# Eight sums of the numerator moved from VectorE to accumulating transfers inside SBUF, in a kernel of attention and a rational MLP

## The chip, the cores and the metric

One core of one Trainium2 chip runs the whole program as one launch. The metric is device microseconds from the start to the end of an execution, the median over the runs shown. The profile is one more execution of the same program, taken with the hardware profiler.

## The reference, cut to what matters

The input is q, k and v of 8 batches, 8 heads, 576 positions and 64 channels. Each head gets a banded attention (a position sees its neighbours at a distance below 4) and a second attention over positions averaged in groups of four; their sum is the MLP's input, 4608 tokens by 512 channels. The MLP has a rational function between its two products:

```python
def _moe_ref(x, w_in, w_out, a, b):
    h = x @ w_in                                   # 4608 x 2048
    h2 = h * h
    h3 = h2 * h
    P = a[0] + a[1] * h + a[2] * h2 + a[3] * h3
    Q = 1.0 + np.abs(b[0]) * np.abs(h) + np.abs(b[1]) * h2
    g = P / (Q + 1e-06)
    return g @ w_out
```

All is float32.

## The kernel before, in words

**The MLP.** The tokens go in nine blocks of 512: one of each batch's first 512 positions, and one of the 64 positions that are left of each batch. A block takes sixteen steps, one for each 128 of the 2048 inner columns, so there are 144 steps, n = 0 to 143; the third block has the steps 32 to 47. A step has three parts:

- TensorE makes h, 128 x 512, in one of two PSUM banks that take turns (line 1090): 12 matmuls, four each of high input with high weights, low input with high weights and high input with low weights. Each float32 factor is split in a high and a low part, so that their three products give the precision of float32.
- `middle` makes g out of h. ScalarE (line 1103) reads the bank four times: |b0 h| into tb, h squared into tq, a3 h + a2 into ta, and a1 h + a0 into u. VectorE makes the denominator, tb = b1 tq + tb (line 1147), and ta = ta tq (line 1152). The last sum of the numerator is ta = ta + u (line 1156). ScalarE takes the logarithm of tb + 1 into log and its negative exponential into tq, which is the reciprocal of the denominator. VectorE then makes the high part gh = ta tq (line 1182), the error of it, tb = (tb + 1) gh (line 1187) and ta = ta - tb (line 1196), and the low part gl = ta tq (line 1182 again).
- `o_part` multiplies g with the output weights into four banks that gather the block's sixteen steps (line 1220): eight matmuls that read gh, with high and low weights in turn, then four that read gl.

Two sets of buffers take turns: even steps use ta = m1, tb = m3, tq = m5, gh = g1, gl = g3; odd steps m0, m2, m4, g0 and g2. u (gb1, gb0) lies in the memory of gh and log (gb3, gb2) in that of gl. So u of step n + 2 waits until TensorE has read gh of step n, and gh of a step is written over its own u.

**Attention for later blocks runs in between.** While a block's MLP runs, the attention of a later batch is worked off in two groups of two head pairs: scores into PSUM (lines 483 and 563 on TensorE), masking (497), maxima (592, 646), exponentials (627, 657 on ScalarE), sums and scaling (668, 669, 674, 692), two transposes on VectorE (779, 759) that go over DRAM and come back as eu and eq, the products with v (932, 894 on TensorE), and the sums into the next block's input (971, 975, 957, 1050). The averages of q, k and v over four positions (pq, vq) are made by transfers: SyncE loads the first of four, and GpSimd's queue adds the other three with accumulating transfers from DRAM (line 444), each of which waits until the one before it on the same tile has landed.

**The order is planned.** Every piece of work is a task with an engine, a planned cost and a due time. A planner in the kernel simulates the five engines, takes on each the most urgent task that is ready, and so writes one fixed order for each engine; the program is emitted in that order, and the engines work it off in order, with semaphores between them. A table of offsets (SHIFT) moves single tasks' due times. An accumulating transfer inside SBUF is already known to the planner through `added`; it stands on GpSimd's queue, with an issue cost of 0.93, a wait of 2.05 and a load of ADD_LOAD = 1.3 in the planner's units:

```python
def added(x, y):
    add(
        "POOL", 0.93, lambda: nc.gpsimd.dma_start(out=x.ap, in_=y.ap, accum_op=ALU.add),
        (x, y), (x,), load=ADD_LOAD,
    )
```

`middle` uses it for the sum of line 1156 in the steps that ADD_DMA names, of which there are none before the change.

Of the kernel before, what the change touches and what calls it, by code (L numbers as in the profile page):

```python
# [76 lines left out]
class Plan:  # L77
# [16 lines left out]
    def add(self, engine, dur, fn, reads=(), writes=(), due=None, load=None, at=0.0, wait=2.05, big=False, more=None):  # L94
        t = Task()
        t.engine, t.dur, t.fn, t.due, t.n, t.load, t.at = engine, dur, fn, due, len(self.tasks), load, at
        t.preds, t.succs, t.late, t.start = {}, [], 1e9, None
        t.key, t.wait, t.big, t.more = self.key, wait, big, more
        self.key = t.key[0], t.key[1] + 1
        rk = set().union(*(r.keys for r in reads)) if reads else set()  # L100
        wk = set().union(*(w.keys for w in writes)) if writes else set()
        for k in rk | wk:
            w = self.writer.get(k)
            if w is not None:
                t.preds[w] = True
        for k in wk:
            for r in self.readers.get(k, ()):
                t.preds.setdefault(r, False)
            self.writer[k] = t
            self.readers[k] = []  # L110
        for k in rk - wk:
            self.readers.setdefault(k, []).append(t)
        t.preds.pop(t, None)
        for p in t.preds:
            p.succs.append(t)
        self.tasks.append(t)
        return t
# [91 lines left out]
def attention_moe(  # L209
# [895 lines left out]
# [5 lines that stand above are left out]
# [26 lines left out]
    def middle(n):  # L1136
# [15 lines left out]
        add("DVE", 0.602, lambda: v.tensor_tensor(out=ta.ap, in0=ta.ap, in1=tq.ap, op=ALU.mult), (ta, tq), (ta,))  # L1152
        if n in ADD_DMA:
            added(ta, u)
# [321 lines left out]
ET_DVE = ()  # L1476
MASK_LATE = 2
POOL_PE = {1: (1, 'ACT')}
ADD_DMA = range(0)
SUB_DMA = range(0)  # L1480
NEG = ()
ADD_LOAD = 1.3
# [261 lines left out]
```

## Time and profile before

| | us |
|---|---|
| median of 2 runs | 942.74 (942.63 to 942.84) |
| span of the profiled execution, first to last instruction | 944.6 |
| TensorE busy in the span | 927.3 |
| VectorE busy | 873.4 |
| ScalarE busy | 772.9 |
| GpSimd busy | 153.1 |

The profiled execution's own time is its span, 944.6 us; no other time of that execution is given, and it lies 1.9 us above the median of the runs. Busy times count an instruction from its start to its end; instructions that overlap in a pipeline have longer durations than distances (a matmul of 512 columns lasts 0.39 us and is followed by the next after 0.23 us), so distances between starts say what an engine can do.

### The profile page before, as it was taken

What the parts mean: (1) busy time and instruction counts of PE and PEld (TensorE: products, weight loads), DVE (VectorE), ACT (ScalarE), POOL (GpSimd) and SP (SyncE); (2) the same over time, 40 slices, a digit from 0 to 9 for tenths busy, and PEclk for the clock granted to TensorE, in tenths of its full rate; (3) what the DMA queues carried; (4) which work ended last, traced back from release to release, by engine and by line L of the source; (5) the groups of instructions that cost most, each with busy time, mean ns of one, the idle gap of its engine ahead of it and who ended that gap; (6) DMA issues with size and microseconds to landing.
All of it is one profiled execution on the core that took longest, in us unless ns stands there. A gap on an engine that the chain in (4) does not pass through costs nothing.

```text
span 944.6 us, 19519 instructions
## 1 busy us (share of the span) xinstructions
PE 927.3 (98%) x7011; PEld 726.4 (77%) x7011; DVE 873.4 (92%) x1549; ACT 772.9 (82%) x1943; POOL 153.1 (16%) x182
## 2 busy tenths in 40 slices
PE   9998999999999999999999999999999999999996
PEld 7655666778777878878787878887878888788885
DVE  6998999999999999999999999999999988988886
ACT  4898999997797979796989788888979776777664
POOL 2032233130302222121203030304020000000000
PEclk9999999999999999999999999999999999999999
DMA  9679855643465646575656565656633010001001
GB/s 284 249 216 245 254 114 90 190 67 116 87 151 123 136 112 140 146 134 124 131 148 116 136 122 157 111 144 112 178 63 91 1 45 1 0 1 45 1 1 45
DMA packets 93136, 109.32 MB, mean 116 GB/s; under 512 B 23120, under 2 KB 75344, under 8 KB 93040
## 3 DMA queue, kind: packets, MB, share of 16 engines
q1 hardware_dynamic: 70000, 88.01, 31.7%
q0 software_dynamic: 23040, 20.07, 15.8%
q8 instruction: 55, 0.90, 0.4%
q14 instruction: 41, 0.34, 0.1%
HBM read 87.05 MB, written 20.99 MB: 114 GB/s over the span
## 4 chain that ended last, share of the span: by engine, by line
PE 44%; DVE 25%; ACT 23%; issue 5%; DMA 1%; SPq 1%; DVEq 0%; ACTq 0%
PE psum L1220 18%; PE psum L1090 16%; ACT m L1103 10%; DVE g L1182 5%; ACT gb L1103 5%; PE psum L1078 4%; ACT el L627 3%; DVE m L1147 3%; DVE m L1152 3%; DVE m L1196 3%; DVE m L1187 3%; ACT ep L674 2%; ACT ep L657 2%; DVE nm L592 1%; DVE xf L957 1%
## 5 line engine op out<-in xcount | busy, mean ns | idle before, releaser
L1220 PE MATMUL psum<-wh,g 128*128 128x512 f32 x1152 | 370.2, 398 | 4.0 <-DVE g L1182 2.6
L1090 PE MATMUL psum<-xs,wh 128*128 128x512 f32 (+1 forms) x1040 | 262.4, 389 | 0.3
L1220 PEld LDWEIGHTS psum<-wh,g 128*128 128x128 f32 x1152 | 213.5, 188 | 60.6 <-DVE g L1182 7.7
L1103 ACT ACTIVATE m<-psum,cf 128x512 f32<-128x512 f32 x288 | 210.8, 743 | 53.0 <-PE psum L1090 41.9
L1090 PEld LDWEIGHTS psum<-xs,wh 128*128 128x128 f32 x1040 | 191.8, 188 | 43.2 <-ACT gb L1103 2.7
L1182 DVE TENSOR_TENSOR g<-m,m 128x512 fp32r<-128x512 f32 x288 | 194.6, 686 | 32.9 <-ACT m L1103 25.2
L1220 PE MATMUL psum<-wl,g 128*128 128x512 f32 x576 | 224.5, 391 | 0.0
L1090 PE MATMUL psum<-xs,wl 128*128 128x512 f32 (+1 forms) x520 | 138.1, 387 | 0.0
L1103 ACT ACTIVATE gb<-m 128x512 f32<-128x512 f32 x144 | 93.0, 646 | 47.7 <-DVE m L1147 39.3
L1220 PEld LDWEIGHTS psum<-wl,g 128*128 128x128 f32 x576 | 108.2, 188 | 21.3
L1103 ACT ACTIVATE gb<-psum,cf 128x512 f32<-128x512 f32 x144 | 114.0, 792 | 7.0 <-PE psum L1220 6.2
L1090 PEld LDWEIGHTS psum<-xs,wl 128*128 128x128 f32 x520 | 96.4, 188 | 20.7 <-issue 1.0
L1147 DVE SCALAR_TENSOR_TENSOR m<-m,cf,m 128x512 f32<-128x512 f32 x144 | 107.0, 743 | 5.4 <-ACT m L1103 4.3
L1103 ACT ACTIVATE m<-gb 128x512 f32<-128x512 f32 x144 | 92.7, 644 | 15.0 <-DVE m L1152 9.4
L444 POOL DMA_DIRECT2D vq<-in_vq_dram x60 | 52.3, 915 | 312.0 <-DMA vq<-in_vq_dram 260.6
L1156 DVE TENSOR_TENSOR m<-m,gb 128x512 f32<-128x512 f32 x144 | 98.6, 685 | 3.9 <-ACT gb L1103 3.1
L444 POOL DMA_DIRECT2D pq<-in_qkp_dram x84 | 73.6, 933 | 174.0 <-DMA pq<-in_qkp_dram 166.7
L1187 DVE SCALAR_TENSOR_TENSOR m<-m,g 128x512 f32<-128x512 f32 x144 | 98.9, 687 | 2.1
L1196 DVE TENSOR_TENSOR m<-m,m 128x512 f32<-128x512 f32 x144 | 98.8, 686 | 1.6
L1152 DVE TENSOR_TENSOR m<-m,m 128x512 f32<-128x512 f32 x144 | 98.4, 683 | 0.9 <-ACT m L1103 0.9
L1103 ACT ACTIVATE m<-psum 128x512 f32<-128x512 f32 x144 | 87.1, 605 | 2.0 <-DVE g L1182 1.6
L627 ACT ACTIVATE el<-el,nm 128x64 f32<-128x64 f32 x240 | 80.6, 350 | 2.6 <-DVE nm L619 2.2
(100 smaller groups left out, 884.2 us busy)
## 6 DMA issues: line engine op xcount, KB each, us to landing
qk<-in_qk_dram SPq DMA_DIRECT2D x32, 590.0 KB, 13.3
pq<-in_qkp_dram POOLq DMA_DIRECT2D x84, 144.0 KB, 3.9
vw<-in_vw_dram SPq DMA_DIRECT2D x32, 320.0 KB
out_dram<-xf SPq DMA_DIRECT2D x32, 256.0 KB, 2.5
bounce<-tt SPq DMA_DIRECT2D x96, 80.0 KB, 1.9
eu<-bounce SPq DMA_DIRECT2D x40, 160.0 KB, 3.2
sl<-in_w_out_dram SPq DMA_DIRECT2D x12, 512.0 KB, 3.6
vq<-in_vq_dram POOLq DMA_DIRECT2D x60, 96.0 KB, 3.1
```

The source lines that it names most:

```text
L444: lambda d=dst, x=src, r=r: nc.gpsimd.dma_start(out=d.ap, in_=rows(x, r), accum_op=ALU.add),
L627: nc.scalar.activation(out=s.el.ap[:, k, j, :], in_=view[:, j, k, :], func=AF.Exp, bias=nm[:, 5 * j + k : 5 * j + k + 1], scale=scale, acc ...
L1078: nc.tensor.matmul(ph.ap, lhsT=bits[0][fc].ap[:, c, :].bitcast(F32), rhs=x.ap[:, c, :], start=(c == 0), stop=(c == NCC - 1),)
L1090: nc.tensor.matmul(ph.ap[:, f * t : (f + 1) * t], lhsT=(high, low)[j][0][fc].ap[:, c, :], rhs=blk.x[i].ap[:, c, t0 : t0 + t], start=(part_ ...
L1103: add("ACT", cost, lambda: nc.scalar.activation(out=out_.ap, in_=in_, func=func, **kw), (room_in, cf, *more), (out_,))
L1147: lambda: v.scalar_tensor_tensor(out=tb.ap, in0=tq.ap, scalar=b1, in1=tb.ap, op0=ALU.mult, op1=ALU.add),
L1152: add("DVE", 0.602, lambda: v.tensor_tensor(out=ta.ap, in0=ta.ap, in1=tq.ap, op=ALU.mult), (ta, tq), (ta,))
L1156: add("DVE", 0.602, lambda: v.tensor_tensor(out=ta.ap, in0=ta.ap, in1=u.ap, op=ALU.add), (ta, u), (ta,))
L1182: return v.tensor_tensor(out=out, in0=x, in1=y, op=ALU.mult)
L1187: lambda: v.scalar_tensor_tensor(out=tb.ap, in0=tb.ap, scalar=CONE, in1=gh.ap.bitcast(F32), op0=ALU.add, op1=ALU.mult),
L1196: add("DVE", 0.602, lambda: v.tensor_tensor(out=ta.ap, in0=ta.ap, in1=tb.ap, op=op), (ta, tb), (ta,))
L1220: nc.tensor.matmul(ob[sub].ap, lhsT=g[i].ap[:, g0 : g0 + P], rhs=flat((high, low)[j][1][fc].ap), start=(fc == 0 and m == 0), stop=(fc == N ...
```

## The change

In the steps 40 to 47, the second half of the third block, ta = ta + u is no longer an instruction of VectorE. GpSimd's queue issues a transfer of 256 KB from u to ta, both in SBUF, that adds to what is there. The planner is run again with these eight tasks on the other engine, and its order changes around them.

```diff
-ADD_DMA = range(0)
+ADD_DMA = range(40, 48)
```

On VectorE eight rows of line 1156 go; on GpSimd's queue eight rows of a new line 1107 come. On all engines the order is the same up to step 40 and, but for a few neighbours that change places between the steps 118 and 123, again from step 55 on.

**GpSimd's queue.** This is where the transfers of the steps 43 to 47 stand between the accumulating loads of line 444 (pq and vq are the averages for the attention, m1 and m0 the numerators ta of even and odd steps, gb1 and gb0 their u):

```order
+L1107 DMA m0_161<-gb0_171 128x512
 L444 DMA vq1_216<-in_vq_dram 128x192
 L444 DMA vq0_215<-in_vq_dram 128x192
...
 L444 DMA vq1_216<-in_vq_dram 128x192
 L444 DMA vq0_215<-in_vq_dram 128x192
+L1107 DMA m1_162<-gb1_172 128x512
+L444 DMA pq1_203<-in_qkp_dram 128x288
+L444 DMA pq0_192<-in_qkp_dram 128x288
+L1107 DMA m0_161<-gb0_171 128x512
```

The transfers of the steps 40 to 43 stand one behind the other ahead of the six loads of vq; that of step 44 stands behind all six, and that of step 45 behind the first two loads of pq. The remaining two stand behind the other four loads of pq.

**VectorE between gh and gl of step 44.** First as it was (g1 and g3 are gh and gl of this even step, m1, m3 and m5 its ta, tb and tq; the other names are of step 45 and of the attention):

```order
L1182 TENSOR_TENSOR g1_168<-m1_162,m5_166 128x512
L592 TENSOR_REDUCE nm1_182<-el1_207 128x10
L497 TENSOR_TENSOR el0_196<-psum,maskd_178 128x128
L619 TENSOR_TENSOR nm1_182<-nm1_182,scales_180 128x10
L1187 SCALAR_TENSOR_TENSOR m3_164<-m3_164,g1_168 128x512
L592 TENSOR_REDUCE nm0_181<-el0_196 128x10
L1152 TENSOR_TENSOR m0_161<-m0_161,m4_165 128x512
L619 TENSOR_TENSOR nm0_181<-nm0_181,scales_180 128x10
L1196 TENSOR_TENSOR m1_162<-m1_162,m3_164 128x512
L1147 SCALAR_TENSOR_TENSOR m2_163<-m4_165,cf_179,m2_163 128x512
L1182 TENSOR_TENSOR g3_170<-m1_162,m5_166 128x512
```

And as it is now:

```order
L1182 TENSOR_TENSOR g1_168<-m1_162,m5_166 128x512
L668 TENSOR_SCALAR sm1_186<-sm1_186 128x13
L1152 TENSOR_TENSOR m0_161<-m0_161,m4_165 128x512
L669 RECIPROCAL sm1_186<-sm1_186 128x13
L1147 SCALAR_TENSOR_TENSOR m2_163<-m4_165,cf_179,m2_163 128x512
L692 TENSOR_TENSOR el1_207<-el1_207,sm1_186 128x640
L759 STREAM_TRANSPOSE tp1_212<-ep1_210 128x480
L1187 SCALAR_TENSOR_TENSOR m3_164<-m3_164,g1_168 128x512
L779 STREAM_TRANSPOSE tt1_204<-el1_207 128x640
L1196 TENSOR_TENSOR m1_162<-m1_162,m3_164 128x512
L1182 TENSOR_TENSOR g3_170<-m1_162,m5_166 128x512
```

The masking and maxima of the attention that stood here have moved ahead of gh, and the scaling and the two transposes that stood behind gl are now in front of it. TensorE's row has moved with it: the second four of the eight products with gh of step 44 stood ahead of the score products of line 563 and of h of step 46 before, now all eight stand behind h of step 46, six ahead of h of step 47 and two behind it.

**ScalarE at step 46.** Before, u of this step (gb1) followed its tb (m3) directly (m5 is tq, gb3 log; m2, m4 and m0 are of step 47, el0 of the attention):

```order
L1103 ACTIVATE m5_166<-psum 128x512
L1103 ACTIVATE m3_164<-psum,cf_179 128x512
L1103 ACTIVATE gb1_172<-psum,cf_179 128x512
L627 ACTIVATE el0_196,sm0_185<-el0_196,nm0_181 128x64 x5
L1103 ACTIVATE gb3_174<-m3_164 128x512
```

Now seven rows stand between them, the first of them ep0's exponential:

```order
L1103 ACTIVATE m3_164<-psum,cf_179 128x512
L657 ACTIVATE ep0_199,sm0_185<-psum,nm0_181 128x144 x3
L1103 ACTIVATE m2_163<-psum,cf_179 128x512
L1103 ACTIVATE gb3_174<-m3_164 128x512
L674 ACTIVATE ep0_199<-ep0_199,sm0_185 128x144 x3
L1103 ACTIVATE m5_166<-gb3_174 128x512
L1103 ACTIVATE m0_161<-psum,cf_179 128x512
L1103 ACTIVATE m4_165<-psum 128x512
L1103 ACTIVATE gb1_172<-psum,cf_179 128x512
```

So the last reading of step 46's PSUM bank, which h of step 48 is written to, now stands behind that step's own logarithm and exponential, behind the scaling of line 674 and behind two readings of step 47's bank.

## Rows read from the trace of the kernel before

**Rows 1.** Windows: stretch, its length, busy us (instructions) by engine, clock, DMA
```profile
core 0: us, PE busy (x) PEld busy (x) DVE busy (x) ACT busy (x) POOL busy (x), PEclk, DMA share, GB/s
321.00:372.00 51.00, 50.77 (x409) 40.92 (x408) 48.73 (x88) 42.99 (x121) 10.50 (x12) 1.00 0.61 134
...
750.00:800.00 50.00, 50.00 (x221) 41.23 (x221) 42.32 (x66) 36.15 (x60) 0.00 (x0) 1.00 0.06 22
```

**Rows 2.** Waits of TensorE's matmuls and weight loads, 321 to 380 us
```profile
PE psum L483 <- DVE el L497: 0.2, 1, 0.2
...
PEld psum L1090 <- ACT gb L1103: 0.4, 1, 0.4
```

**Rows 3.** Line 1156 in 321 to 372 us: durations, first and last start
```profile
L1156 DVE TENSOR_TENSOR m<-m,gb x8: 684/686/692, 324.5 to 367.4; 128x512 f32<-128x512 f32 x8
```

**Rows 4.** DMA issues of the whole span: KB each, median us to landing
```profile
pq<-in_qkp_dram POOLq DMA_DIRECT2D x84, 144.0 KB, 3.9
...
out_dram<-xf SPq DMA_DIRECT2D x32, 256.0 KB, 2.5
...
vq<-in_vq_dram POOLq DMA_DIRECT2D x60, 96.0 KB, 3.1
```

**Rows 5.** Line 444, 300 to 400 us: landing, min, median, max
```profile
DMA to landing us min/median/max: 2.8/3.6/5.8
```

**Rows 6.** Timeline of ScalarE at step 40: start, duration
```profile
322.31 0.79 ACT L1103 ACTIVATE gb<-psum,cf 128x512 f32<-128x512 f32 x1
```

**Rows 7.** Timeline of VectorE at the steps 40 and 41
```profile
324.47 0.69 DVE L1156 TENSOR_TENSOR m<-m,gb 128x512 f32<-128x512 f32 x1
...
326.40 0.65 DVE L1182 TENSOR_TENSOR g<-m,m 128x512 fp32r<-128x512 f32 x1
326.97 0.74 DVE L1147 SCALAR_TENSOR_TENSOR m<-m,cf,m 128x512 f32<-128x512 f32 x1
327.62 0.68 DVE L1187 SCALAR_TENSOR_TENSOR m<-m,g 128x512 f32<-128x512 f32 x1
328.23 0.69 DVE L1152 TENSOR_TENSOR m<-m,m 128x512 f32<-128x512 f32 x1
```

**Rows 8.** Timeline of TensorE at the steps 40 and 41
```profile
327.48 0.39 PE L1220 MATMUL psum<-wh,g 128*128 128x512 f32 x1
...
329.29 1.98 PE L1090 MATMUL psum<-xs,wh 128*128 128x512 f32 x8
...
332.01 1.30 PE L1220 MATMUL psum<-wh,g 128*128 128x512 f32 x5
```

**Rows 9.** Timeline of GpSimd's queue, the six loads of vq
```profile
342.60 1.76 POOL L444 DMA_DIRECT2D vq<-in_vq_dram  x2 [24.01 <-PE psum L894]
...
351.73 0.89 POOL L444 DMA_DIRECT2D vq<-in_vq_dram  x1 [0.35 <-issue]
```

**Rows 10.** Timeline of TensorE at h of step 47, behind that of step 46
```profile
355.99 2.11 PE L1090 MATMUL psum<-xs,wh 128*128 128x512 f32 x8
```

**Rows 11.** Timeline of VectorE: scaling and transposes of the attention
```profile
357.53 0.83 DVE L692 TENSOR_TENSOR el<-el,sm 128x640 f32<-128x640 f32 x1
358.27 0.69 DVE L1182 TENSOR_TENSOR g<-m,m 128x512 fp32r<-128x512 f32 x1
358.87 0.84 DVE L779 STREAM_TRANSPOSE tt<-el 128x640 f32<-128x640 f32 x1
359.63 0.63 DVE L759 STREAM_TRANSPOSE tp<-ep 128x480 f32<-128x480 f32 x1
```

**Rows 12.** Timeline of ScalarE: line 674, log, exponential, ta, u
```profile
358.08 1.04 ACT L674 ACTIVATE ep<-ep,sm 128x144 f32<-128x144 f32 x3
...
362.37 0.66 ACT L1103 ACTIVATE gb<-m 128x512 f32<-128x512 f32 x1
...
363.46 0.66 ACT L1103 ACTIVATE m<-gb 128x512 f32<-128x512 f32 x1
363.98 0.81 ACT L1103 ACTIVATE m<-psum,cf 128x512 f32<-128x512 f32 x1
...
365.12 0.81 ACT L1103 ACTIVATE gb<-psum,cf 128x512 f32<-128x512 f32 x1
```

**Rows 13.** Windows: TensorE before and in its slow stretch
```profile
74.00:78.00 4.00, 1.75 (x5) 0.44 (x3) 3.57 (x8) 4.00 (x16) 2.97 (x3) 1.00 0.80 187
78.50:81.50 3.00, 2.73 (x25) 2.01 (x26) 0.99 (x2) 0.43 (x1) 0.00 (x0) 0.50 0.97 281
```

## Prediction

> **What bounds the kernel now.** I read first the windows. From 321 to 372 us, the stretch in which the eight sums run, TensorE is busy 50.77 of 51.00 us and VectorE 48.73 [rows 1]. Both look full, and a busy share alone doesn't tell which is the bound. The second row does: from 750 to 800 us no attention is left, VectorE is busy 42.32 of 50 us, and TensorE passes 221 matmuls in 50.00 us, one each 0.226 us. TensorE keeps the same pace where it is fed without fail, so this is its own pace, and 24 matmuls make 5.4 us a step whatever VectorE does. Then I read who waits in the stretch: TensorE's matmuls wait 0.2 us, once, and its weight loads at most 0.4 us at one place on ScalarE [rows 2]. So TensorE is the bound of this stretch, VectorE runs close behind, and the reader is to see that work taken off VectorE meets nothing that waited for VectorE. The sum lies in all eight steps (a count of 8 between 324.5 and 367.4 us [rows 3]). I make the working against the profiled execution, 944.6 us, and carry the difference over to the median, 942.74, which lies 1.9 us below it.
>
> **What the change removes.** Eight instructions of 0.686 us [rows 3]. They overlap their neighbours: the row starts at 327.62 and 328.23 are 0.61 us apart [rows 7], so VectorE gets back 8 x 0.61 = 4.9 us. By rows 2 there is nearly nothing for which TensorE waits on VectorE, and I count this gain as 0.6 us, the waits of rows 2.
>
> **What it adds: a landing.** gh of a step now waits for a transfer that adds 256 KB inside SBUF, from GpSimd's queue. The trace has none of that kind. Bounds from the nearest rows: a plain transfer of 256 KB to DRAM lands 2.5 us after its issue, the low end; the accumulating loads of the same queue take 3.1 us for 96 KB and 3.9 us for 144 KB, and the line through these two gives 3.9 + 112 x 0.8 / 48 = 5.8 us for 256 KB, the high end [rows 4], which is also the longest of line 444 between 300 and 400 us [rows 5]. I take 4.3 us: the row with the same queue and the same kind of work, 3.9, and a little for more bytes.
>
> The Trainium skill, DMA: Bandwidth & Descriptors, section Anatomy of one DMA — SWDGE (gpsimd) path, fits a DMA of this queue as about 2.0 us and its bytes at 436 GB/s. By that 256 KB land in 2.6 us, and 144 KB in 2.3, where rows 4 show 3.9; the rows decide. By 2.6 us the first three terms below would nearly vanish and the sum would be about 4.6 instead of 7.6.
>
> **The path, step by step.** "Before" is the trace; each later step carries the delays of the ones ahead of it.
>
> Step 40. u is ready at 322.31 + 0.79 = 323.1 [rows 6]. The transfer lands at 327.5 with 0.1 for the semaphore, where the sum on VectorE allowed gh to start at 326.40 [rows 7]. gh lasts 0.65, so TensorE can begin at 328.25. It began at 327.48 [rows 8] directly behind other matmuls. Wait: 0.8 us.
>
> Step 41. Behind the later gh, ta tq starts 0.57 + 0.65 + 0.61 = 1.83 us after 327.5 [rows 7], ends at 330.0, the transfer lands at 334.4, gh ends at 335.1. TensorE wanted it at 332.01 + 0.9 = 332.9, behind the four products with gl of step 40 [rows 8]; it is now 0.8 late and has four matmuls of h of step 44 in front, 0.9 more, which makes 334.6. Wait: 0.5 us.
>
> Steps 42 and 43. The new order puts the attention's products ahead of theirs, about 3 us of work, and I find no wait. Cost 0; without this cover it would be as in step 41, 0.5 each.
>
> Step 44. The transfer stands on GpSimd's queue behind the six loads of vq. They are released by the attention's products (line 894), the last is issued at 351.73 and takes 0.89 [rows 9], and those products come 0.4 later now. So the transfer is issued at 353.0 whatever its operands do, lands at 357.3, and gh, which was made at 349.0, ends at 358.05. TensorE reaches it behind h of step 46: that ended at 355.99 [rows 10], by when four of the eight products with gh of step 44 had been made that now come later, so 355.99 - 0.9 + 1.3 = 356.4. Wait: 1.7 us.
>
> gl of step 44. Between gh and gl VectorE's row now holds five full tiles (about 3.1 us), the scaling of line 692 and the transposes 779 and 759, 0.74 + 0.76 + 0.6 [rows 11], and two small ones, 0.2 each: 5.4 us. gl ends at 357.4 + 5.4 + 0.7 = 363.5. TensorE has 20 matmuls until then, 4.5 us from 358.1: 362.6. Wait: 0.9 us.
>
> gl of step 45. It stands eight rows on, 4.35 us, and ends at 367.85; TensorE, after the four with gl of step 44 and eight with gh, is there at 366.2. Wait: 1.6 us. The transfer of step 45 should have landed by its gh at 363.4.
>
> h of step 48. Its bank is free when ScalarE has made u of step 46, which now stands behind the logarithm, line 674, the exponential, ta and squares of step 47. tb of step 46 ends at 367.2 by the same row of VectorE; then 0.66 for the logarithm, 0.95 for line 674 with its own start, 0.66 for the exponential, and 365.12 + 0.81 - 363.98 = 1.95 for ta, square and u [rows 12]: 371.5. TensorE is ready at 367.85 + 0.9 = 368.75. Wait: 2.7 us.
>
> Behind this TensorE has 24 matmuls of h without a wait, in which VectorE and ScalarE catch up, and from step 55 on the order is the old one. TensorE doesn't get lost time back where it is the bound. Sum: 0.8 + 0.5 + 1.7 + 0.9 + 1.6 + 2.7 = 8.2, less 0.6 of old waits: 7.6 us. Of these, 3.0 hang on the landing and 5.2 on the order alone. Predicted: 942.7 + 7.6 = 950.3 us, 0.8% more. A measurement of this kernel can tell about 2%, or 18.9 us, from no change, so the forecast counts as no change.
>
> With a landing of 2.5 us the first two terms go and the third falls to nothing, 3.0 less, and the last three come out earlier by what VectorE gained, perhaps 2 more: +2.5. With 5.8 us the five steps that are exposed (40, 41, 44, 45 and 46) lose 1.5 each: +15.
>
> **Rivals.** *The landings are hidden.* For it: the planner put other work in front of the products, and VectorE has 4.9 us less to do in 51. Against: three terms come from the order and not from the landing. If VectorE is ahead by its 4.9 us when it comes to step 44, the last three terms fall to about 1: 942.7 + 1, some 944.
>
> *VectorE is the bound.* For it: 48.73 busy of 51.00 [rows 1]. Then the 4.9 us come off: 937.8. Against: rows 2, and a faster VectorE can take off only what TensorE waits, 0.6.
>
> *The landing is long* (the other side: slower by over 2%). Place: gh of the eight steps, behind the transfer. Price: 1 us in each exposed step for each us beyond 4.3, so 5 for each us. To add 18.9 - 7.6 = 11.3 us it must last 4.3 + 2.3 = 6.6 us; from there it decides, and 7 us would give 942.7 + 7.6 + 13.5 = 963.8. For it: 61% of the DMA engines are busy in this stretch already [rows 1], and 256 KB inside SBUF both read and add. Against: the longest landing of line 444 around the stretch is 5.8 [rows 5].
>
> A smaller thing on top of the forecast: after a gap of TensorE in which 4 us held 1.75 busy, its granted clock was 0.50, the level of 1.2 GHz, for the window 78.5 to 81.5 [rows 13]. If the wait at step 48 does the same, some 3 us at half speed add about 1.5; the range holds it.
>
> **How the numbers follow.** Forecast, a loss of 2.5 to 15 us: 0.62. Landings hidden, within 2.5 us of 942.7: 0.22. VectorE the bound: 0.06. Long landing, over 18.9 us: 0.08. The remaining 0.02 I split between both ends. The low end, 942, leaves out the gain and a little of the hidden case; the high end, 959, holds the high bound of the landing with the clock and leaves out the long one. Faster by over 2% needs four times what VectorE gets back, 0.01; slower by over 2% 0.08 + 0.01 = 0.09; the same 0.90.
>
> **What would show it.** Landings of the new line 1107 between 3.6 and 5 us; TensorE waiting on gh (VectorE, line 1182) at the steps 40, 41 and 44, on gl at 44 and 45, and on ScalarE's u at h of step 48, together about 8 us from 325 to 380 and nothing new after that; the transfer of step 44 issued behind the last vq, past 352 us. If the spans of the block after the third differ from the old ones, or VectorE's idle time ahead of gh is not there, I am wrong on the mechanism; if only a wait on the landing is there and none on the order, I am wrong on the last three terms.

## The result and the profile after

The changed kernel takes 956.47 us (2 runs, 955.19 and 957.74) against 942.74; the ratio is 1.0143, 95% interval 1.0125 to 1.0161. That is no change by the bound of 2%, but the interval lies above 1: the kernel has become about 13.7 us slower. The prediction said no change at 950.3, with 942 to 959 as its range. The profiled execution spans 956.0 us (before 944.6).

The windows of the stretch and of the last 50 us with full work, of the kernel after; columns as in [rows 1]:

```profile
321.00:372.00 51.00, 42.84 (x366) 32.54 (x364) 39.71 (x74) 38.94 (x111) 15.79 (x18) 0.99 0.74 156
750.00:800.00 50.00, 50.00 (x250) 40.99 (x249) 43.29 (x71) 35.63 (x60) 0.00 (x0) 1.00 0.06 22
```

Against [rows 1] TensorE stands still for 8.2 of the 51 us where it had 0.2, and VectorE's busy time falls by 9.0, although only 4.9 us of work were taken off it: VectorE now waits too. From 750 to 800 us TensorE is as full as before. Of line 1156 there are 136 sums left; the eight new ones have this entry, by line (the second row is GpSimd's issue of the transfer, not the transfer):

```profile
L1107 POOLq EVENT_SEMAPHORE  x8: 17/2637/7102, 316.2 to 372.7; - x8
L1107 POOL DMA_DIRECT2D m<-gb x8: 859/866/1221, 322.5 to 373.7; - x8
...
DMA to landing us min/median/max: 3.3/4.2/6.6
```

The landing I took was 4.3 us; the median is 4.2. Next the waits by pair of engines from 321 to 395 us, that is who waited, for whom, us in total, times, longest; it answers to [rows 2]:

```profile
DVE g L1182 <- DMA m<-gb: 8.4, 3, 5.1
...
PE psum L1220 <- DVE g L1182: 4.6, 4, 1.9
...
PE psum L1090 <- ACT gb L1103: 2.6, 1, 2.6
...
PE psum L1220 <- DVE sm L668: 1.5, 1, 1.5
```

VectorE's gh waits for landings, and TensorE waits for VectorE's g, for ScalarE's u (gb) and once for a g that the view puts down to line 668, the row just behind it on VectorE (g ends at 368.60 us, TensorE goes on at 368.74). Each of these waits can be found in TensorE's timeline; the bracket at a row's end is the idle time ahead of it and what ended it:

```profile
325.72 1.07 PE L1090 MATMUL psum<-xs,wl 128*128 128x512 f32 x4
327.77 0.50 PE L1220 MATMUL psum<-wh,g 128*128 128x512 f32 x1 [0.99 <-DVE g L1182]
...
335.63 0.50 PE L1220 MATMUL psum<-wh,g 128*128 128x512 f32 x1 [1.22 <-DVE g L1182]
...
358.90 0.50 PE L1220 MATMUL psum<-wh,g 128*128 128x512 f32 x1 [1.88 <-DVE g L1182]
...
364.27 1.42 PE L1220 MATMUL psum<-wh,g 128*128 128x512 f32 x5 [0.51 <-DVE g L1182]
...
368.74 1.16 PE L1220 MATMUL psum<-wh,g 128*128 128x512 f32 x4 [1.46 <-DVE sm L668]
372.46 3.78 PE L1090 MATMUL psum<-xs,wh 128*128 128x512 f32 x8 [2.56 <-ACT gb L1103]
376.04 1.91 PE L1090 MATMUL psum<-xs,wl 128*128 128x512 f32 x4
377.75 2.23 PE L1090 MATMUL psum<-xs,wh 128*128 128x512 f32 x8
```

They are gh of steps 40, 41 and 44, gl of 44 and 45, and h of step 48. The last matmul ahead of a wait is drawn 0.16 us longer than the distance to its next would be: the first row's four end at 326.79, but at 0.228 us each the next would start at 326.63. So each wait costs 0.16 more than its bracket: 1.15, 1.38, 2.04, 0.67, 1.62 and 2.72 us, 9.6 in all. The last three rows show one more loss: the twelve matmuls of h of step 48 take from 372.46 to 377.75, 5.29 us, where twelve at 0.228 take 2.74. The windows there, with TensorE's granted clock in the third column from the end:

```profile
368.00:372.00 4.00, 1.16 (x4) 0.68 (x4) 3.37 (x7) 4.00 (x9) 0.00 (x0) 0.92 1.04 230
372.00:376.00 4.00, 3.54 (x8) 2.81 (x9) 1.13 (x2) 2.22 (x4) 1.73 (x2) 0.50 1.00 265
376.00:380.00 4.00, 4.00 (x14) 3.17 (x13) 1.69 (x3) 0.00 (x0) 0.00 (x0) 0.72 0.87 182
```

TensorE was busy 1.16 of 4 us, and then its clock stood at 0.50, the 1.2 GHz level. A mean of 0.92, 0.50 and 0.72 over three times 4 us is (0.08 + 0.50 + 0.28) x 4 / 0.5 = 6.9 us at that level. With the matmuls of step 49 that still fall into it, the slow stretch costs 2.8 us.

Does that make up the whole? The last product of step 55, from where the order is the old one, ends at 423.83 us before and at 435.69 after, and h of step 38 started 0.84 us earlier after, so the stretch between costs 12.7 us. Six waits and the clock are 9.6 + 2.8 = 12.4. Nothing comes to it later: of the 11.9 us that step 55 is late, 11.4 are left at the end of the span, 956.0 less 944.6.

That the spans differ by 11.4 us and the medians by 13.7 is scatter between executions, a good part of it from ahead of the change. Wherever both are given, an execution's time is 1.7 to 2.2 us above its span, so the profiled execution of before took some 946.4 us and lay 3.7 above its median; that of the changed kernel, 957.74, lay 1.3 above. Ahead of h of step 38 all thirteen kernels of this document have the same rows on every engine, and yet it starts between 297.9 and 305.5 us in their profiles. So for the experiments I also count from there to the end of the span, one profile each: before it is 944.6 - 302.36 = 642.2 us, after 956.0 - 301.52 = 654.5, which is 12.2 more.

### The profile page after: what moved, and what is told of

It reads as the page before. It is cut to its first block, busy times and chain, and to the rows that moved or that the text cites. A ratio compares the mean times of both kernels' runs of the same rounds, so it can differ in the third digit from the quotient of the medians.

```text
span 956.0 us, 19533 instructions
## 1 busy us (share of the span) xinstructions
PE 930.0 (97%) x7011; PEld 727.6 (76%) x7011; DVE 870.0 (91%) x1541; ACT 772.7 (81%) x1943; POOL 161.0 (17%) x190
## 4 chain that ended last, share of the span: by engine, by line
PE 23%; DVE 20%; ACT 16%; issue 4%; DMA 2%; POOL 0%; DVEq 0%; SPq 0%; ACTq 0%; POOLq 0%
PE psum L1090 11%; PE psum L1220 11%; ACT m L1103 7%; DVE g L1182 5%; ACT gb L1103 4%; DVE m L1147 3%; ACT el L627 3%; DVE m L1196 3%; DVE m L1152 3%; DVE m L1187 3%; ACT ep L674 1%; ACT ep L657 1%; DVE xs L1050 1%; DMA m<-gb 1%; DVE m L1156 1%
## 5 line engine op out<-in xcount | busy, mean ns | idle before, releaser
L1156 DVE TENSOR_TENSOR m<-m,gb 128x512 f32<-128x512 f32 x136 | 92.9, 683 | 3.1 <-ACT gb L1103 2.5
```

## The experiments

My theory when they began: three parts add up, the landing at steps 40, 41 and 44, the moved rows at 44, 45 and 48, and the fall of the clock behind the last wait. The rivals: it is the landing alone; it is the order alone; or VectorE was the bound. The kernel before, measured again beside these runs, took 942.91, 942.95 and 943.23 us.

**No sums at all.** The order of before, with the eight sums gone; their tasks stay in the plan and emit nothing (... stands for the rest of the line):

```diff
-add("DVE", 0.602, lambda: v.tensor_tensor(...), ...)
+add("DVE", 0.602, (lambda: None) if n in range(40, 48) else (lambda: v.tensor_tensor(...)), ...)
```

> The kernel before in its own order, with the eight sums of steps 40 to 47 left out and nothing in their place (so the numerators of these steps lack the term u). It bounds what the change could ever have gained, with no transfer and no moved row. My theory (TensorE sets the pace of this stretch and VectorE's row has room in it): the eight sums stood beside TensorE's work, so the time is 942.1 to 942.9 us, at most 0.6 us under before. Rival, VectorE is the bound there: eight times 0.6 us goes, about 4.9 us, 937.8 us.

Measured: 943.04 us, ratio 1.0001 (0.9988 to 1.0014). The stretch by windows:

```profile
321.00:372.00 51.00, 51.00 (x410) 41.28 (x410) 45.06 (x82) 43.37 (x119) 10.49 (x12) 1.00 0.58 129
```

VectorE has 82 instructions instead of 88 here (eight sums are gone, and two other rows now fall into the window) and 3.7 us less to do, TensorE is as busy as it was, and the time doesn't move. VectorE is not the bound, and the eight sums had nothing to give: in this order no transfer, however fast, could have gained more than the 0.1% that this measurement leaves open.

**The new order without transfers.** In the changed kernel, at the same places of all rows; each sum stands in VectorE's row where the program issued its transfer:

```diff
-nc.gpsimd.dma_start(out=x.ap, in_=y.ap, accum_op=ALU.add)
+nc.vector.tensor_tensor(out=x.ap, in0=x.ap, in1=y.ap, op=ALU.add)
```

> The changed kernel's rows on every engine, but the eight sums are VectorE operations again, at the place in VectorE's row at which the transfer's issue was free of its inputs; no transfer. It tells the moved rows from the landing. My theory has both at work: the landings of steps 40, 41 and 44 (1.15, 1.38 and 2.04 us of TensorE's waits in the changed kernel) go, and with them a part of the 0.67 and 1.62 us behind step 44, while ScalarE's u of step 46, late in its row, still holds up h of step 48 (2.72 us) and the granted clock falls once more behind that wait (2.8 us more): 2 to 6 us over before, 945 to 949 us. Rival 1, the order alone makes the loss: 9 to 14 us over before, 952 to 957 us. Rival 2, the landing alone makes it: within 1 us of before.

Measured: 954.27 us (951.63 to 959.72), ratio 1.0127 (1.0090 to 1.0164). That is rival 1, the order alone, and not what I expected. TensorE's waits from 321 to 395 us, and the four of them in its timeline:

```profile
PE psum L1090 <- ACT gb L1103: 2.5, 1, 2.5
PE psum L1220 <- DVE g L1182: 1.6, 2, 0.9
PE psum L1220 <- DVE sm L668: 1.5, 1, 1.5
```

```profile
356.60 1.21 PE L1220 MATMUL psum<-wh,g 128*128 128x512 f32 x4 [0.67 <-DVE g L1182]
...
365.10 1.43 PE L1220 MATMUL psum<-wh,g 128*128 128x512 f32 x5 [0.91 <-DVE g L1182]
...
369.57 1.17 PE L1220 MATMUL psum<-wh,g 128*128 128x512 f32 x4 [1.46 <-DVE sm L668]
373.29 3.78 PE L1090 MATMUL psum<-xs,wh 128*128 128x512 f32 x8 [2.55 <-ACT gb L1103]
```

The waits at gh of steps 40, 41 and 44 are gone with the transfers. A new one of 0.67 + 0.16 = 0.83 stands ahead of them at gl of step 43 (four matmuls with high weights alone): on VectorE this gl now stands behind the sum of step 44, which starts at 355.26, and ends at 356.54. Of the three that are left none is shorter (1.07, 1.62 and 2.71 us with the 0.16), and h of step 48 again takes 5.29 us. I had thought that they would shrink when gh of step 44 came earlier. They don't, since everything comes earlier together: counted from h of step 38 (301.52 us in the changed kernel, 305.54 here) gh of step 44 is multiplied 3.4 us earlier, gl of step 45 and h of step 48 3.2 us earlier each. So in this order the landing costs 3.2 us by the trace up to h of step 48 (2.4 up to the end, 2.2 by the medians), and the order costs the rest: from h of step 38 to the end it is 9.8 us over before. A small part of this, the 0.83 at gl of step 43 above all, is the sums' own place on VectorE; the new order with the sums left out was not run. The four times scatter over 8 us; the profiled one has a second slow stretch of the clock, before step 40, where its rows are still those of before.

**The transfers without the new order.** In the kernel before, at the same places of all rows, for n from 40 to 47:

```diff
-v.tensor_tensor(out=ta.ap, in0=ta.ap, in1=u.ap, op=ALU.add)
+nc.gpsimd.dma_start(out=ta.ap, in_=u.ap, accum_op=ALU.add)
```

> The rows of the kernel before on every engine, only that the eight sums of steps 40 to 47 are accumulating transfers issued by GpSimd, with no room made for their landing. My theory: a landing of 4.2 us stands in every one of the eight steps between ScalarE's u and VectorE's g of the high part, against 0.8 to 2.3 us that the row leaves; TensorE waits some 2 to 3 us in each step and more in step 44, whose transfer stands behind vq loads on GpSimd's queue: 15 to 25 us over before, 958 to 968 us, and more if the clock falls behind several of these waits. Rival, the planner's new order is what costs and the landing is hidden: 0 to 3 us over before, 943 to 946 us.

Measured: 965.43 us, ratio 1.0239 (1.0223 to 1.0254), 22.5 us more, as expected. TensorE's waits from 321 to 395 us, and the landing of the eight:

```profile
PE psum L1220 <- DVE g L1182: 8.8, 6, 2.8
PE psum L894 <- DVE xf L957: 4.0, 1, 4.0
PE psum L1090 <- ACT gb L1103: 1.2, 1, 1.2
```

```profile
DMA to landing us min/median/max: 3.3/4.2/4.7
```

The second row is worth a look: TensorE waits 4.0 us for a small sum of the attention, line 957, that has nothing to do with the transfers. On VectorE it stands behind gh of step 43, which waits 4.4 us for its landing. Not all of the 22.5 us is waiting: the granted clock falls behind three of these waits (0.57 from 334 to 338 us, 0.72 from 350 to 356, 0.57 from 382 to 386), for 10 us at 1.2 GHz in all. So the planner's new order does hide much of the landings: 22.5 us in the old order, 2 to 3 in the new one. But making the room costs some 10 us itself.

**Which row of the new order costs.** The longest wait is that of h of step 48 for u of step 46. In the changed kernel only this moves on ScalarE (the row in words):

```diff
 |b0 h| of step 46
+u of step 46
 three rows of line 657, |b0 h| of step 47
 log of step 46, line 674, exp of step 46, ta and square of step 47
-u of step 46
```

> The changed kernel with one ScalarE instruction moved: u of step 46 stands directly behind the absolute value |b0 h| of its step, five ScalarE rows earlier (ahead of three scalings of the next block and four activations of step 47). My theory: h of step 48 no longer waits 2.72 us for its bank, TensorE's clock does not fall behind it (6.8 us at half speed in the changed kernel, 2.8 us of loss), so 4.5 to 6 us under the changed kernel, 950.5 to 952 us. Rival 1, the clock's fall has nothing to do with this wait: only the wait goes, 2 to 3 us, 953.5 to 954.5 us. Rival 2, the time is only passed on, because the landings of the sums of steps 46 and 47 (5.4 and 6.6 us), which the slow stretch now hides, come out: within 1.5 us of the changed kernel.

Measured: 956.39 us (953.36 to 957.77), ratio 1.0138 (1.0116 to 1.0159): rival 2, nothing gained. The wait is not gone but elsewhere; TensorE's timeline, then VectorE's ahead of it:

```profile
370.87 2.11 PE L1090 MATMUL psum<-xs,wh 128*128 128x512 f32 x8 [0.37 <-ACT gb L1103]
...
378.42 2.01 PE L1220 MATMUL psum<-wh,g 128*128 128x512 f32 x5 [2.73 <-DVE g L1182]
```

```profile
373.79 0.69 DVE L1196 TENSOR_TENSOR m<-m,m 128x512 f32<-128x512 f32 x1
377.07 1.29 DVE L1182 TENSOR_TENSOR g<-m,m 128x512 fp32r<-128x512 f32 x2 [2.58 <-DMA m<-gb]
```

The second row of VectorE is gh of step 47 and behind it gl of step 46. gh waits for the landing of step 47's sum, and gl, which was ready at 374.5, stands behind it. In the changed kernel the landings of steps 46 and 47 are the longest of the eight, 5.4 and 6.6 us, and cost nothing there, as TensorE is busy with its slow matmuls until 380.7. Once u is early, they are what is late next. The clock falls here too, behind the new wait: 0.63 from 378 to 382 us and 0.94 from 382 to 386, 3.4 us at 1.2 GHz. From h of step 38 to the end it is 12.7 us over before, where the changed kernel has 12.2.

So the same move is made where there is no landing: the kernel with the new order and the sums on VectorE, with u of step 46 moved in the same way.

> The changed kernel's rows with the eight sums back on VectorE (as in e_order), and ScalarE's u of step 46 directly behind the absolute value of its step. With no landing left that could come out behind it, the move shows what the place of u alone cost. Theory A (one wait of 2.7 us of TensorE and the fall of its granted clock behind it, 2.8 us): about 5.5 us under e_order's 954.3, 947.5 to 950 us. Theory B (the wait goes, the clock falls elsewhere): 2.7 us under, 951 to 952 us. Theory C (another wait takes its place, as the landing of step 46 did in e_u46): within 1 us of e_order, 953.3 to 955.3 us.

Measured: 948.16 us (947.43 to 950.12), ratio 1.0050 (1.0035 to 1.0066), 6.1 us under the same order without the move: theory A. The four waits left are 0.67, 0.96, 1.42 and 0.48 us long by their brackets, and the clock stays at 1.00 behind them. Put together:

| median us | sums on VectorE | sums as transfers |
|---|---|---|
| order of before | 942.9 | 965.4 |
| new order | 954.3 | 956.5 |
| new order, u of step 46 early | 948.2 | 956.4 |

Counted from h of step 38 to the end, the rows read 0 and 21.8, 9.8 and 12.2, 5.1 and 12.7 us over before. The transfers cost 8.2 us in the last row and 2.2 in the one above; the late u costs 6.1 without transfers (4.7 from h of step 38) and nothing with them. The late u and the landings lie over each other: each is paid when the other is taken away, and together they cost no more than the landings alone.

**The clock.** In the kernel with the new order and the sums on VectorE, 11 matmuls are put in front of h of step 48, which keep TensorE busy while it waits:

```diff
+for c in range(11):
+    nc.tensor.matmul(banks[0].ap, lhsT=high[0][15].ap[:, c % 4, :], rhs=xs[0][0].ap[:, c % 4, :], ...)
 h of step 48
```

> As e_order, with 11 matmuls 128x512 more on TensorE ahead of h of step 48, whose result nothing reads; at 0.21 to 0.24 us each they fill the wait of 2.72 us for u of step 46. The wait stays as long, only TensorE is busy in it. Theory A (the granted clock falls because TensorE stands idle there): the clock stays at 1.00 in the stretch behind, 2.8 us are saved, 950.5 to 952 us. Rival (the clock's fall has another cause, or the matmuls push h of step 48 later than its wait did): 954 us or more.

Measured: 951.03 us (949.82 to 952.81), ratio 1.0078 (1.0054 to 1.0103), 3.2 us under the same order without them: theory A. TensorE's timeline, where line 1442 is the 11 matmuls, and the window behind them:

```profile
365.16 1.17 PE L1220 MATMUL psum<-wh,g 128*128 128x512 f32 x4 [1.42 <-DVE sm L668]
366.17 2.66 PE L1442 MATMUL psum<-xs,wh 128*128 128x512 f32 x11
368.89 2.11 PE L1090 MATMUL psum<-xs,wh 128*128 128x512 f32 x8
370.84 1.07 PE L1090 MATMUL psum<-xs,wl 128*128 128x512 f32 x4
371.74 1.98 PE L1090 MATMUL psum<-xs,wh 128*128 128x512 f32 x8
```

```profile
369.00:373.00 4.00, 4.00 (x18) 3.31 (x19) 3.83 (x7) 1.66 (x3) 0.00 (x0) 1.00 0.73 212
```

h of step 48 starts as late as it did, but its twelve matmuls take 2.85 us (368.89 to 371.74) and not 5.29: the clock stays at 1.00, the 2.4 GHz level. From h of step 38 to the end it is 6.9 us over before, 2.9 less than without them. So it was TensorE's idleness in front of step 48 that brought the clock down, and a wait of 2.7 us there costs 2.8 more behind it. With early u, 2.72 + 2.8 = 5.5 were expected; 6.1 were measured by the medians and 4.7 from h of step 38.

Such a wait doesn't always bring the clock down. Near 76 us, where the rows of both kernels are the same, TensorE stands still for 3.02 us in the profile of before and for 2.91 in that of the changed kernel. This is the place of [rows 13]; before first, then after:

```profile
74.00:82.00 8.00, 4.98 (x31) 2.73 (x30) 5.06 (x12) 5.13 (x18) 2.97 (x3) 0.79 0.90 232
74.00:82.00 8.00, 5.09 (x35) 2.60 (x34) 5.89 (x14) 5.95 (x22) 3.29 (x3) 1.00 0.92 247
```

TensorE is busy nearly as long, and the clock falls in one execution and not in the other. What decides this was not tried.

**Step 44's place on GpSimd's queue.** In the changed kernel (the row in words):

```diff
 four loads of vq
+transfer of step 44
 two loads of vq
-transfer of step 44
```

> The changed kernel with the transfer of step 44 two places earlier on GpSimd's queue, ahead of the last two loads of vq instead of behind them. In the changed kernel it was issued at 354.05, directly behind the last vq load, while its own operand (the product ta tq of step 44) was ready at 352.55. My theory (the queue holds it up): it is issued about 1.4 us earlier, and the wait of TensorE for gh of step 44 falls from 2.04 to between 0.6 and 1.2 us (in e_order, without any transfer, 0.83 us of it stayed). What is left of this in the whole time is small, 0 to 1.5 us, as the later waits of steps 45 to 48 can take it up. Rival (the operands or the landing hold it, not the queue): the wait stays at 2 us.

Measured: 953.82 us (952.57 to 954.07), ratio 1.0116 (1.0101 to 1.0131). GpSimd's timeline in the changed kernel, then here, and TensorE at gh of steps 41 and 44 here:

```profile
353.51 0.86 POOL L444 DMA_DIRECT2D vq<-in_vq_dram  x1 [0.21 <-issue]
354.05 1.22 POOL L1107 DMA_DIRECT2D m<-gb  x1
```

```profile
350.39 0.86 POOL L1107 DMA_DIRECT2D m<-gb  x1 [1.91 <-issue]
...
332.95 0.50 PE L1220 MATMUL psum<-wh,g 128*128 128x512 f32 x1 [1.98 <-DVE g L1182]
...
354.79 0.50 PE L1220 MATMUL psum<-wh,g 128*128 128x512 f32 x1 [0.44 <-DVE g L1182]
```

The wait is 0.44 + 0.16 = 0.60 instead of 2.04: it was the queue, as predicted. (The 0.83 us that the expectation compares this with was the wait at gl of step 43.) By the medians the whole gains about 2.6 us on the changed kernel, each beside its own runs of before. The profile doesn't bear this out: from h of step 38 to the end it is 12.1 us over before, against 12.2. Of the 1.4 us won at step 44, 0.9 are lost at steps 40 and 41, whose waits are 1.32 and 2.14 here (the transfer of step 41 landed in 5.2 us, not 4.4), and a new wait of 0.55 + 0.16 = 0.71 us comes at 378.79. So the gain of 2.6 isn't shown to come from the move.

**A longer landing told to the planner.**

```diff
-ADD_LOAD = 1.3
+ADD_LOAD = 2.3
```

> The changed kernel with the landing that the planner reckons with raised by 1.0 us, to some 4.35 us, near the 4.2 us measured. Theory landing (TensorE waits at steps 40, 41 and 44 because the planner was told 3.35 us): these waits shrink by up to 1 us each and their rows are planned around, 951 to 954 us. Theory order (what costs is that the planner moves rows to make room, and it now moves more): 956 to 961 us.

Measured: 957.53 us, ratio 1.0144 (1.0115 to 1.0172). TensorE's waits from 315 to 400 us:

```profile
PE psum L1220 <- DVE g L1182: 3.6, 5, 1.5
PE psum L1090 <- ACT gb L1103: 3.0, 3, 1.6
PE psum L563 <- DVE el L497: 1.4, 1, 1.4
```

The waits at gh of steps 40 and 41 shrink from 1.15 and 1.38 to 0.62 and 0.75, as a better known landing should do, though the landings were longer here (4.4 to 5.7 us, median 5.0) than what the planner was told. What is won there is lost at other places: three waits for ScalarE's u, one at the scores of the attention, and two more of 1.1 and 1.5 us behind 400 us.

**Two steps only.**

```diff
-ADD_DMA = range(40, 48)
+ADD_DMA = range(40, 42)
```

> The change for steps 40 and 41 alone, six sums stay on VectorE. In the changed kernel these two steps cost TensorE 1.15 and 1.38 us of wait and nothing else by then. Theory landing: the same two waits, 2 to 3 us over before, 945 to 946 us. Theory order (the loss comes from rows moved at steps 44 to 48, where the transfers meet the scalings and the vq loads of the next block): 943 to 944 us. Above 947 us the planner has moved other rows too, and the landing isn't what decides.

Measured: 958.59 us, ratio 1.0158 (1.0128 to 1.0189). Neither theory's number: two transfers cost as much as eight. TensorE's waits from 315 to 400 us:

```profile
PE psum L1220 <- DVE g L1182: 5.4, 4, 1.6
```

Two of the four are gh of steps 40 and 41, 1.81 and 1.53 us, and the rest is from a plan that is another one from here to far behind: TensorE stands still for 6.8 us between 300 and 400 us and for 5.1 between 400 and 600, against 0.3 and 0.2 before.

**Other orders, no transfer at all.** So I asked what any new plan costs. The kernel before, all sums on VectorE, with the planned cost of the eight sums a tenth higher (shown) or lower, 0.542:

```diff
-add("DVE", 0.602, ...)
+add("DVE", 0.662 if 40 <= n < 48 else 0.602, ...)
```

> No transfer and nothing taken off VectorE: the kernel before, only that the planner is told 0.662 instead of 0.602 for the eight sums of steps 40 to 47 and so writes another order from step 40 on. It asks whether it is the transfers at all that the new order suffers from. Theory transfers (the order of the changed kernel is bad because the planner must make room for landings): this order is as good as before, 941 to 945 us. Theory any new order (the order before is a good one among many that the planner's rules can give, and a small change of a cost draws another): 947 to 958 us without a single transfer.

> As e_cost_up, with 0.542 told for the eight sums. Theory transfers: 941 to 945 us. Theory any new order: 947 to 958 us, and not the same as e_cost_up, since the two orders differ.

Measured: 945.86 us, ratio 1.0031 (1.0017 to 1.0045) with 0.662, and 951.97 us, ratio 1.0091 (1.0070 to 1.0111) with 0.542. The first misses both expectations by a little, between "as good as before" and "any new order"; the second is the latter. TensorE's timeline in the second:

```profile
362.72 2.78 PE L1090 MATMUL psum<-xs,wh 128*128 128x512 f32 x8 [2.47 <-ACT gb L1103]
365.29 1.91 PE L1090 MATMUL psum<-xs,wl 128*128 128x512 f32 x4
367.00 2.14 PE L1090 MATMUL psum<-xs,wh 128*128 128x512 f32 x8
```

The very pattern of the changed kernel, without a transfer in the program: h waits 2.5 us for a u that the planner put late on ScalarE, and the twelve matmuls behind take 4.28 us where 2.74 would do. So a late u and the clock's fall behind it can come with an order of this planner without any landing; the other of these two orders has no such wait.

No kernel here beats the one before, and the kernel without any sums shows that in its order moving these eight cannot. Whether the planner has a better order somewhere was not searched.

## Why the prediction was right, and where its sizes were off

**The range** held, the size did not: the loss was 13.7 us where 7.6 was forecast. That 956.5 still lies below 959 is in part luck, since that end was built from a landing of 5.8 us with the clock on top, and the loss came from the order and the clock at a median landing of 4.2.

**What bounds the kernel** held: without the eight sums nothing is gained. The 0.6 us counted as gain was not there either, by the medians (943.04 against 942.91).

**The landing** held in the median, 4.2 with 4.3 taken, but not in its spread: it was to lie between 3.6 and 5 us, and three of the eight lay outside, 3.3 at step 42, 5.4 and 6.6 at steps 46 and 47.

**The six waits** came at the six places, and none came at steps 42 and 43:

| | predicted | measured |
|---|---|---|
| gh of step 40 | 0.8 | 1.15 |
| gh of step 41 | 0.5 | 1.38 |
| gh of step 44 | 1.7 | 2.04 |
| gl of step 44 | 0.9 | 0.67 |
| gl of step 45 | 1.6 | 1.62 |
| h of step 48 | 2.7 | 2.72 |

The term most off is step 41's. The working let the transfer start when the product ta tq ended. GpSimd's timeline in the changed kernel:

```profile
330.43 0.87 POOL L1107 DMA_DIRECT2D m<-gb  x1 [7.02 <-ACT m L1103]
```

The product ended at 329.58, so 0.85 us lie between, and the wait came out 0.9 longer. The row names ScalarE's exponential of that step, which ended shortly before the issue but is no operand of the transfer. At step 40, where u was the last operand, it was 0.3 us from its end at 322.24 to the issue at 322.54. What fills these times I have not tried; I counted nothing for them. Two sums of the working are off by a little: gh of step 40 ends at 328.15, not 328.25, and the row between gh and gl of step 44 adds up to 5.6 us, not 5.4. Neither changes the argument.

**The clock** was the largest miss. The prediction named it as a smaller thing on top, some 3 us at half speed for 1.5 us, taken from [rows 13]. It was 6.9 us at half speed and 2.8 us. It was also left out of the predicted time, though the wait that it hangs on was one of the six terms. Waits 9.6 instead of 8.2 and 2.8 for the clock make the 12.4 of the trace; the medians say 13.7, and their two runs lie 2.5 us apart.

**The split** into 3.0 for the landing and 5.2 for the order came out as 4.6 and 5.0 in the waits of the changed kernel. What failed is the sentence built on it, that with a landing of 2.5 us the last three terms would come out earlier and leave 2.5. Without any landing the new order still costs about 11 (8.5 to 15.5 by the interval, 9.8 from h of step 38). Taking a wait of TensorE away moves VectorE, ScalarE and TensorE behind it by the same time, and the later waits stay. The rival *the landings are hidden*, at 944, rested on the same step and falls with it.

***The landing is long*** came true at two steps, 5.4 and 6.6 us at 46 and 47, in windows in which the DMA engines are full (1.04, 1.00 and 0.87 above). It did not decide, because the late u and the slow clock covered just these two; with u early, that of step 47 (4.9 us there) came out at once as 2.73 us of wait. Over the transfers themselves the DMA share was 0.46 to 0.64 for the three that landed in 3.3 to 3.6 us, 0.82 to 0.97 for the three of 4.0 to 4.4, and 1.03 and 0.92 for these two. That full DMA engines make a landing long fits this, but was not tried.

**What stays open**: why the planner puts u late. The runs show that it does so with and without transfers, and that this and the clock behind it are the largest single loss. Open is also which rows cause the 5 us that remain of the new order with u early: its four waits make 4.2 of them, with the 0.16 each, and the rows ahead of them were not moved one by one.

## What to carry to other kernels

Before work is moved off an engine, take it out altogether and time that: here it gave 0.1 us, and no transfer can beat leaving out. Where a planner writes the order, a change has two prices, its own and that of the new plan; measure the new plan with the old operation and the old plan with the new operation, since here they were 11 and 22 us, and 14 together. Two delays that lie over each other hide one another, so a fix of one that gains nothing doesn't show that it was free.

## What the runs showed of the hardware that was not expected

- A wait of TensorE of 2.7 us cost 2.8 us more behind it, at a granted clock of 0.50 for 6.9 us; 11 matmuls without use in the wait, 2.66 us, kept the clock at 1.00 and gained 3.2 us of the whole. At another place the same rows stood still for 3.02 us in one execution and the clock fell, and for 2.91 in another and it stayed at 1.00.
- An accumulating transfer of 256 KB inside SBUF landed in 3.3 to 4.7 us in the old order and in 3.3 to 6.6 in the changed kernel, where a plain one of that size to DRAM took 2.5 [rows 4].
- Between the end of a transfer's last operand and the start of its issue on GpSimd lay 0.3 us where the operand came from ScalarE, and 0.53, 0.70 and 0.85 in the steps 42, 45 and 41, where VectorE made it.
